# Prefetch hints on the closing branches, a shorter wait list on SyncE, and a row-sum check in two parts

## The chip, the cores and the metric

The kernel runs on one core of one Trainium2 chip. The metric is the device time of one execution in microseconds (us). Ratios below are the ratio of runs to the kernel before in the same comparison, with a 95% interval; they are not quite the ratio of the medians quoted beside them.

Terms: TensorE (PE, and PEld for its weight loads), VectorE (DVE), ScalarE (ACT), GpSimd (POOL) and SyncE (SP) are each given a program of their own. A "q" behind an engine's name in the profile means its sequencer: branches, waits, loads of registers. A P·V step multiplies the softmax weights by V (tile `ps_o`), a projection multiplies the result by `wo` (tile `ps_pj`), and a partial sum adds a projection to what was summed before; the last one of each half goes to the output buffer `ost`.

## The reference

Two attention layers side by side, their outputs concatenated:

```python
def _A_ref(x, k_cache, v_cache, wq, wo):        # 32 query heads share 4 key/value heads
    q = (x @ wq).reshape(B, Sq, Hq, Dh).transpose(0, 2, 1, 3)
    k, v = jnp.repeat(k_cache, rep, axis=1), jnp.repeat(v_cache, rep, axis=1)
    p = softmax(einsum("bhqd,bhkd->bhqk", q, k) * Dh ** -0.5)
    return einsum("bhqk,bhkd->bhqd", p, v).transpose(0, 2, 1, 3).reshape(B, Sq, Hq * Dh) @ wo
# _B_ref: the same with 32 key/value heads. B=16, Sq=32, D=1024, Sk=1024, Dh=128, bfloat16
return concatenate([a, b], axis=-1)
```

## The kernel before

The kernel holds two programs. The fast one computes softmax without subtracting the row maximum and records the reciprocal of every row sum in `rinv_all`. At its end a check asks whether all of these lie between 1e-10 and 1e10. If not, a general program computes everything again. With these inputs the check always passes, so every engine jumps over the general program, which lies between its fast program and the end.

The check, as it stands at the end of the fast program (cut):

```python
pr.add("dve", ... tensor_scalar(chk[:], rinv_all[:], RINV_LOW, None, ALU.is_ge, ALU.min, accum_out=good[:, 0:1]))
pr.add("dve", ... tensor_scalar(chk[:], rinv_all[:], RINV_HIGH, None, ALU.is_le, ALU.min, accum_out=good[:, 1:2]))
pr.add("pe",  ... matmul(ps_pj[0:1, 0:2], ones[:], good[:], start=True, stop=True))   # bank of the projections
pr.add("dve", ... tensor_tensor(good[0:1, 0:1], ps_pj[0:1, 0:1], good[0:1, 0:1], ALU.mult))
pr.add("dve", ... tensor_tensor(good[0:1, 1:2], ps_pj[0:1, 1:2], good[0:1, 0:1], ALU.mult))
pr.add("dve", ... tensor_copy(flag[:], good[0:1, 1:2]))
```

The closing of every engine's program:

```python
def whole(name, eng):
    fast.run_engine(name, eng, fast_sems)
    eng.wait_ge(fast_sems[flag_op.eng], flag_op.sig)
    reg = eng.alloc_register("flag_" + name)
    eng.reg_load(reg, flag[0:1, 0:1])
    if name == "sp":
        fast.await_dmas(eng, fast_sems)          # one wait for each of the DMA semaphores
    with eng.If_ne(reg, flag_good):
        ...                                      # meet the other engines, run the general program
```

The output goes out in eight stores of 128x1024 through one buffer `ost`, filled in two halves:

```python
pr.add("dve", ... tensor_tensor(o_ap, a_ap, ps_pj[:, 0:OUTW], ALU.add), writes=[BK_PJ, "ost"], name="accF")
...
pr.add("sp", ... dma_start(out_flat[...], ost[:, :]), reads=["ost"], dma_key=f"out{pi}")
```

The order on each engine is not the order of the source. A list scheduler reorders the whole fast program by the longest path to its end, so a changed check at the end can move instructions far ahead of it.

## Time and profile before

| | before |
|---|---|
| three runs | 858.39, 861.65, 861.66 us |
| span of the profiled run | 857.6 us |
| bytes moved, 0 to 820 us | 405 GB/s |
| bytes moved, 820 us to the end | 261 GB/s |
| last store issued | 851.72 us |
| last store issued to end of span | 5.88 us |

The body is bound by transfers (405 GB/s up to 820 us; the DMA engines stand at 9 tenths in 39 of the page's 40 slices); the change lies in the last six microseconds. The timeline there (start, duration, engine, line, operation, output from input, and in brackets the idle time before and what ended it):

```profile
851.00 0.69 DVE L725 TENSOR_TENSOR ost<-acc,ps_pj 128x512 bf16<-128x512 f32 x1 [1.70 <-PE ps_pj L709]
851.72 0.36 SPq L728 DMA_DIRECT2D out_dram<-ost  x1
...
851.75 0.19 PE L1108 MATMUL ps_pj<-good,ones 128*1 128x2 f32 x2 [0.78 <-DVE ost L725]
...
852.34 0.14 DVE L1114 CAST flag<-good 1x1 int32<-1x1 f32 x1
```

The check runs after the last store was issued, and the flag is there at 852.48. What follows is not engine work, so it is not in the timeline. It is in the view of single source lines (engine, operation, count, shortest/median/longest in ns, first and last start in us). The line of the branch:

```profile
L364 ACTq COMPARE_BRANCH  x1: 45/45/45, 853.3 to 853.3; - x1
L364 POOLq COMPARE_BRANCH  x1: 45/45/45, 853.3 to 853.3; - x1
L364 DVEq COMPARE_BRANCH  x1: 76/76/76, 853.3 to 853.3; - x1
L364 PEldq COMPARE_BRANCH  x1: 3648/3648/3648, 853.4 to 853.4; - x1
L364 SPq COMPARE_BRANCH  x1: 50/50/50, 854.5 to 854.5; - x1
```

SyncE's list of waits, the reason that its branch is 1.2 us later than the others:

```profile
L341 SPq EVENT_SEMAPHORE  x20: 28/28/28, 853.3 to 854.4; - x20
```

The first instruction behind the branch, a drain at the end of the block:

```profile
L355 POOLq DRAIN  x1: 41/41/41, 853.5 to 853.5; - x1
L355 ACTq DRAIN  x1: 80/80/80, 856.7 to 856.7; - x1
L355 DVEq DRAIN  x1: 57/57/57, 857.0 to 857.0; - x1
L355 PEldq DRAIN  x1: 73/73/73, 857.1 to 857.1; - x1
L355 SPq DRAIN  x1: 59/59/59, 857.3 to 857.3; - x1
```

The gap between branch and drain: 0.2 us on GpSimd, 2.8 to 3.7 us on the four others. On TensorE it is recorded as a long branch, on the others as nothing at all between two short instructions. I read the gap as a wait for the instructions of the branch target: packets of the instruction queues begin 0.9 to 1.1 us after these branches, 8 KB at 854.20, 854.40 and 855.45 us and 16 KB at 854.36. What the engines wait for in the rest of the gap the trace does not show.

The last store landed after 2.03 us. Its transfer, in the DMA view from issue to landing (40 slices of the stretch):

```profile
DMA  0000000000000000079799698996974200000000
GB/s 0 0 0 0 0 0 0 0 0 0 0 0 0 0 0 0 40 282 444 282 444 484 242 484 323 404 484 242 484 282 162 81 0 0 0 0 0 0 0 0
...
out_dram<-ost SPq DMA_DIRECT2D x1, 256.0 KB, 2.0
```

### The profile page before, as it was taken

Reading aid. Unit: us, or ns where it says so; the run is one execution under the profiler, and the core shown is the slowest. Engines: PE = TensorE matmul, PEld = TensorE weight load, DVE = VectorE, ACT = ScalarE, POOL = GpSimd, SP = SyncE. Lnnn points to the kernel's source line nnn. Section 1 sums busy time; section 2 is a strip of 40 time slices with the busy share of each in tenths; the row PEclk is TensorE's granted clock in tenths of the full one; section 3 lists DMA queues with packets and bytes.
Section 4 is the critical chain, followed back from the end, with each engine's and each line's share of the span. In section 5 each row is a group of like instructions: output and inputs, shape, how many; then the busy total and the mean of one; then the engine's idle time right before and its main releaser. Section 6 shows DMA issues by size and latency. Waiting matters only on the chain.

```text
span 857.6 us, 27298 instructions
## 1 busy us (share of the span) xinstructions
PE 717.3 (84%) x11970; PEld 436.2 (51%) x12098; DVE 541.5 (63%) x1115; ACT 447.1 (52%) x981; POOL 67.9 (8%) x76
## 2 busy tenths in 40 slices
PE   3999998898978789888897979988889778878885
PEld 2546655455545455555554545545455445545452
DVE  1655566666657477577674756757777656666674
ACT  1456766466544464546554545544565554555452
POOL 0001000100000000000000000000000000000000
PEclk9999999999999999999999989999999999999898
DMA  9999999999999999999999999999999999999994
GB/s 341 366 400 412 413 412 389 413 415 399 413 400 385 413 410 412 402 400 411 403 412 404 406 411 401 411 408 408 413 403 412 412 409 412 414 411 409 411 384 174
DMA packets 135547, 341.57 MB, mean 398 GB/s; under 512 B 10496, under 2 KB 26880, under 8 KB 119040
## 3 DMA queue, kind: packets, MB, share of 16 engines
q1 hardware_dynamic: 135424, 339.78, 101.1%
q8 instruction: 96, 1.57, 0.7%
q14 instruction: 27, 0.22, 0.1%
HBM read 337.64 MB, written 2.10 MB: 396 GB/s over the span
## 4 chain that ended last, share of the span: by engine, by line
DMA 53%; PE 19%; DVE 15%; SPq 6%; issue 4%; ACT 2%; POOL 1%; POOLq 0%; DVEq 0%
DMA KB_sb<-in_B_k_cache_dram 40%; DVE KBt_sb L820 12%; DMA VA_sb<-in_A_v_cache_dram 5%; PE ps_pj L709 4%; PE ps_s L855 3%; DMA woA_sb<-in_A_wo_dram 3%; PE ps_pj L651 3%; PE ps_pj L668 2%; SPq L800 2%; PE ps_o L947 2%; PE ps_kt L913 2%; SPq L682 1%; PE ps_s L838 1%; PE ps_pt L897 1%; DMA woB_sb<-in_B_wo_dram 1%
## 5 line engine op out<-in xcount | busy, mean ns | idle before, releaser
L820 DVE STREAM_TRANSPOSE KBt_sb<-KB_sb 128x1024 f32<-128x1024 f32 x256 | 306.1, 1226 | 97.7 <-DMA KB_sb<-in_B_k_cache_dram 93.9
L878 ACT ACTIVATE P_sb<-ps_s 128x512 bf16<-128x512 f32 x256 | 152.4, 600 | 84.1 <-PE ps_s L855 74.5
L870 ACT ACTIVATE PTA_sb<-ps_s 128x1024 bf16<-128x1024 f32 x128 | 131.3, 1026 | 104.2 <-PE ps_s L838 91.5
L855 PE MATMUL ps_s<-KBt_sb,QB_sb 32*32 32x512 bf16 x4096 | 146.9, 395 | 10.1 <-DVE KBt_sb L820 5.5
L582 ACT COPY PT_sb<-ps_pt 128x512 f32<-128x512 f32 x128 | 74.9, 585 | 105.7 <-PE ps_o L947 88.6
L794 POOL COPY VAp_sb<-VA_sb 128x1024 bf16<-128x1024 bf16 x64 | 66.6, 1041 | 761.9 <-DMA VA_sb<-in_A_v_cache_dram 729.4
L897 PE MATMUL ps_pt<-id,P_sb 128*128 128x128 f32 x512 | 105.5, 305 | 9.3 <-ACT P_sb L878 7.3
L947 PE MATMUL ps_o<-VB_sb,PT_sb 128*32 128x128 bf16 x4096 | 81.6, 221 | 23.7 <-DMA VB_sb<-in_B_v_cache_dram 16.6
L897 PEld LDWEIGHTS ps_pt<-id,P_sb 128*128 128x128 f32 x512 | 82.7, 206 | 35.2 <-ACT P_sb L878 17.7
L947 PEld LDWEIGHTS ps_o<-VB_sb,PT_sb 128*32 128x32 bf16 x4096 | 60.0, 97 | 60.2 <-issue 56.9
L913 PE MATMUL ps_kt<-VAp_sb,PTA_sb 128*128 128x129 bf16 x1024 | 80.8, 222 | 10.9 <-POOL VAp_sb L794 4.9
L913 PEld LDWEIGHTS ps_kt<-VAp_sb,PTA_sb 128*128 128x128 bf16 x1024 | 67.5, 99 | 36.5 <-POOL VAp_sb L794 14.9
L838 PE MATMUL ps_s<-QT_sb,KTA_sb 128*128 128x256 bf16 x512 | 82.2, 275 | 3.0 <-DVE KTA_sb L584 2.0
L855 PEld LDWEIGHTS ps_s<-KBt_sb,QB_sb 32*32 32x32 bf16 x4096 | 49.3, 90 | 60.9 <-DVE KBt_sb L820 10.6
L709 PE MATMUL ps_pj<-woA_sb,OTA_sb 128*128 128x512 bf16 x224 | 64.0, 394 | 17.4 <-DMA woA_sb<-in_A_wo_dram 10.0
L963 DVE TENSOR_SCALAR OB_sb<-ps_o,rinv_all 128x128 bf16<-128x128 f32 x128 | 43.7, 342 | 53.4 <-PE ps_o L947 52.6
L709 PE MATMUL ps_pj<-woB_sb,OTB_sb 128*128 128x512 bf16 x206 | 62.0, 394 | 16.6 <-ACT OTB_sb L582 4.5
L668 PE MATMUL ps_pj<-xT_sb,wq_sb 128*128 128x512 bf16 x234 | 64.2, 389 | 8.4 <-DMA wq_sb<-in_B_wq_dram 3.4
L651 PE MATMUL ps_pj<-xT_sb,wq_sb 128*128 128x512 bf16 x232 | 63.9, 380 | 8.3 <-DMA wq_sb<-in_A_wq_dram 4.1
L883 DVE TENSOR_TENSOR stat<-stat 64x1 f32<-64x1 f32 x256 | 41.9, 164 | 32.0 <-ACT P_sb L878 24.4
L838 PEld LDWEIGHTS ps_s<-QT_sb,KTA_sb 128*128 128x128 bf16 x512 | 45.0, 98 | 25.5 <-issue 4.4
L722 DVE TENSOR_TENSOR acc<-acc,ps_pj 128x512 f32<-128x512 f32 x64 | 43.0, 672 | 20.1 <-PE ps_pj L709 19.7
(49 smaller groups left out, 533.0 us busy)
## 6 DMA issues: line engine op xcount, KB each, us to landing
KB_sb<-in_B_k_cache_dram SPq DMA_DIRECT2D x128, 1024.0 KB, 9.1
VB_sb<-in_B_v_cache_dram SPq DMA_DIRECT2D x256, 512.0 KB, 9.8
KA_sb<-in_A_k_cache_dram SPq DMA_DIRECT2D x64, 256.0 KB, 10.3
VA_sb<-in_A_v_cache_dram SPq DMA_DIRECT2D x64, 256.0 KB, 9.6
wq_sb<-in_B_wq_dram SPq DMA_DIRECT2D x32, 256.0 KB, 8.6
wq_sb<-in_A_wq_dram SPq DMA_DIRECT2D x32, 256.0 KB, 8.5
woB_sb<-in_B_wo_dram SPq DMA_DIRECT2D x32, 256.0 KB, 10.8
woA_sb<-in_A_wo_dram SPq DMA_DIRECT2D x32, 256.0 KB, 10.1
```

Of the source, the lines that this page charges most:

```text
L582: pr.add("act", lambda e: e.copy(dst_ap, src_ap), reads=reads, writes=writes, name=name + "@act", wtag=wtag, rtag=rtag)
L651: last = e.matmul(ps_pj[:, 0:tn], wq_sb[:, 0, j, hc * Dh:(hc + 1) * Dh], xT_sb[:, 0, j, t0:t0 + tn], start=(j == 0), stop=(j == DJ - 1))
L668: last = e.matmul(ps_pj[:, 0:NTOK], w, xT_sb[:, 1, j, :], start=(j == 0), stop=(j == DJ - 1))
L709: last = e.matmul(ps_pj[:, 0:OUTW], OT[:, gp, hh, :], wo_[:, hh, oh * OUTW:(oh + 1) * OUTW], start=(hh == 0), stop=(hh == nh - 1))
L820: pr.add("dve", lambda e: e.transpose(KBt_sb[:, sl, t_, :].bitcast(F32).rearrange("p (s r i) -> p s r i", r=2, i=32), KB_sb[:, rs, t_, :]. ...
L838: last = e.matmul(ps_s[:, sbf, c2, i * 2 * P:(i + 1) * 2 * P], KTA_sb[:, sl, c * P:(c + 1) * P], qt, start=True, stop=True)
L855: last = e.matmul(ps_s[32 * cg:32 * cg + 32, sbf, g, :].rearrange("p (sh cl j) -> p sh cl j", sh=4, cl=4), lhsT, kt[32 * a:32 * a + 32, g, ...
L870: pr.add("act", lambda e: e.activation(dst, src, ACTF.Exp, scale=scale), writes=BK_S[sbf] + [("PTA", q.half)], name="expA", rtag={("Sv", s ...
L878: pr.add("act", lambda e, src=src, dst=dst, g=g: e.activation(dst, src, ACTF.Exp, scale=scale, accum_out=st[:, g:g + 1]), writes=[BK_S[sbf ...
L897: last = e.transpose(ps_pt32[:, m * P:(m + 1) * P], p32[:, m:Sk // 2:NPK], id32[:])
L913: last = e.matmul(ps_kt[:, qh * OA0:qh * OA0 + Dh + 1], PTA_sb[:, h, c, qh * P:(qh + 1) * P], VAp_sb[:, sl, 4 * h + c, 0:Dh + 1], start=(h ...
L947: last = e.matmul(ps_o[32 * a:32 * a + 32, 0:Dh], PT_pairs[:, c // 2, 32 * (a ^ (c // 4 * 2)):32 * (a ^ (c // 4 * 2)) + 32, c % 2], VB_sb[ ...
```

## The change

Its intent is to shorten the end: fetch the branch target ahead, let SyncE branch before it waits for the stores (and only for these), and have the flag ready before the last partial sums.

```diff
+NLATE = 8
-    def run_engine(self, eng_name, eng, sems):
+    def run_engine(self, eng_name, eng, sems, mark=None):
+        mine = [op for op in self.ops if op.eng == eng_name]
+        for k, op in enumerate(mine):
+            if mark is not None and k == max(0, len(mine) - mark[0]):
+                mark[1]()
...
+    stored = [k for k in sorted(fast.dma_count) if k.startswith("out")]
+    ahead = {"sp": 6, "pe": 60, "act": 12, "dve": 14, "pool": 3}
...
-            fast.run_engine(name, eng, fast_sems)
+            hints = []
+            fast.run_engine(name, eng, fast_sems, (ahead[name], lambda: hints.append(eng.mark_branch_hint_location())))
             eng.wait_ge(fast_sems[flag_op.eng], flag_op.sig)
             ...
-            if name == "sp":
-                fast.await_dmas(eng, fast_sems)
-            with eng.If_ne(reg, flag_good):
+            eng.br_ne(reg, flag_good, on_true=again, on_false=after).branch_hint(hints[0])
+            with nc.body(again, valid_engines=[eng.engine]):
+                if name == "sp":
+                    fast.await_dmas(eng, fast_sems, stored)
                 ...
+                eng.br(after)
+            nc.switch_bb(after)
+            if name == "sp":
+                fast.await_dmas(eng, fast_sems, stored)
...
+        # st_check_early, at step NIT - NLATE: the two comparisons over the columns of the first 120 steps
+        # st_check, at the end: the two comparisons over the last 8 steps, then
+                for k_ in range(4):
+                    last = e.matmul(ps_kt[0:1, 448:449], ones[:], good[:, k_:k_ + 1], start=(k_ == 0), stop=(k_ == 3))
+            pr.add("dve", lambda e: e.tensor_copy(flag[:], ps_kt[0:1, 448:449]), reads=[BK_KT], writes=["flag"], name="flag")
-            # one matmul into ps_pj, two products on VectorE, copy to the flag
-        emit_programs(nc, outer, pr, general, flag, P * P)
+        emit_programs(nc, outer, pr, general, flag, 4 * P)
```

`ahead` counts operations before the end of an engine's fast program.

More of the change, by code (lines that the diff above doesn't have):

```diff
@@ L325, in sem_names @@
         return ["pe", "act", "dve", "pool"] + sorted(self.dma_count.keys())
-    def run_engine(self, eng_name, eng, sems):
-        for op in self.ops:
-            if op.eng != eng_name:
-                continue
+    def run_engine(self, eng_name, eng, sems, mark=None):
[3 more added lines that the diff above has]
+                mark[1]()
             for key, val in op.waits:
@@ L337, in run_engine, with await_dmas @@
                 last.then_inc(sems[op.eng], 1)
-    def await_dmas(self, eng, sems):
-        for k, c in sorted(self.dma_count.items()):
-            eng.wait_ge(sems[k], 16 * c)
+    def await_dmas(self, eng, sems, keys):
+        for k in keys:
+            eng.wait_ge(sems[k], 16 * self.dma_count[k])
 def emit_programs(nc, stack, fast, general, flag, flag_good):
@@ L361, in whole @@
             eng.reg_load(reg, flag[0:1, 0:1])
-            if name == "sp":
-                fast.await_dmas(eng, fast_sems)
-            with eng.If_ne(reg, flag_good):
+            again, after = "again_" + name, "after_" + name
+            eng.br_ne(reg, flag_good, on_true=again, on_false=after).branch_hint(hints[0])
+            with nc.body(again, valid_engines=[eng.engine]):
+                if name == "sp":
+                    fast.await_dmas(eng, fast_sems, stored)
                 eng.drain().then_inc(meet, 1)
@@ L368, in whole @@
                 if name == "sp":
-                    general.await_dmas(eng, general_sems)
+                    general.await_dmas(eng, general_sems, sorted(general.dma_count))
+                eng.br(after)
+            nc.switch_bb(after)
+            if name == "sp":
+                fast.await_dmas(eng, fast_sems, stored)
         block.sync(lambda e: whole("sp", e))
@@ L531, in build @@
         chk = sb("chk", [P, 2 * NIT], BF)
-        good = sb("good", [P, 2], F32)
+        good = sb("good", [P, 4], F32)
         ones = sb("ones", [P, 1], F32)
@@ L973, in st_otr, with st_check, e_count, st_check_early @@
                  rtag={"OTps": q.qid}, wtag={("OTv", 1, gp): (q.m, q.G)} if q.last_of_group else None)
+        def st_check():
+            every = [("rinv_all", 0), ("rinv_all", 1)]
+            pr.add("pool", lambda g: g.memset(ones[:], 1.0), writes=["ones"], name="c0")
+            view = rinv_all[:, :].rearrange("p (i t) -> p i t", i=2)
+            outv = chk[:, :].rearrange("p (i t) -> p i t", i=2)
+            for k_, (bound, op) in enumerate(((RINV_LOW, ALU.is_ge), (RINV_HIGH, ALU.is_le))):
+                pr.add("dve", lambda e, k_=k_, bound=bound, op=op: e.tensor_scalar(outv[:, :, NIT - NLATE:], view[:, :, NIT - NLATE:], bound, None, op, ALU.min,
+                                                                               accum_out=good[:, 2 + k_:3 + k_]),
+                       reads=every, writes=["chk", ("good", 2 + k_)], name="check")
+            def e_count(e):
+                for k_ in range(4):
+                    last = e.matmul(ps_kt[0:1, 448:449], ones[:], good[:, k_:k_ + 1], start=(k_ == 0), stop=(k_ == 3))
+                return last
+            pr.add("pe", e_count, reads=["ones"] + [("good", k_) for k_ in range(4)], writes=[BK_KT], name="check")
+            pr.add("dve", lambda e: e.tensor_copy(flag[:], ps_kt[0:1, 448:449]), reads=[BK_KT], writes=["flag"], name="flag")
+            pr.add("pool", lambda g: g.memset(ones[:], 1.0), reads=["flag"], writes=["ones"], name="c0")
+        def st_check_early():
+            view = rinv_all[:, :].rearrange("p (i t) -> p i t", i=2)
+            outv = chk[:, :].rearrange("p (i t) -> p i t", i=2)
+            for k_, (bound, op) in enumerate(((RINV_LOW, ALU.is_ge), (RINV_HIGH, ALU.is_le))):
+                pr.add("dve", lambda e, k_=k_, bound=bound, op=op: e.tensor_scalar(outv[:, :, 0:NIT - NLATE], view[:, :, 0:NIT - NLATE], bound, None, op, ALU.min,
+                                                                               accum_out=good[:, k_:k_ + 1]),
+                       reads=[("rinv_all", 0), ("rinv_all", 1)], writes=["chk", ("good", k_)], name="check")
         quadsA = [mk_quadA(t) for t in range(NIT)]
@@ L1097, in build @@
             lazy_pop(LAZY_PER_STEP)
+            if t == NIT - NLATE:
+                st_check_early()
         cur_step[0] = 10 ** 9
         lazy_pop(1000)
-        def st_check():
-            every = [("rinv_all", 0), ("rinv_all", 1)]
-            pr.add("pool", lambda g: g.memset(ones[:], 1.0), writes=["ones"], name="c0")
-            pr.add("dve", lambda e: e.tensor_scalar(chk[:], rinv_all[:], RINV_LOW, None, ALU.is_ge, ALU.min, accum_out=good[:, 0:1]),
-                   reads=every, writes=["chk", ("good", 0)], name="check")
-            pr.add("dve", lambda e: e.tensor_scalar(chk[:], rinv_all[:], RINV_HIGH, None, ALU.is_le, ALU.min, accum_out=good[:, 1:2]),
-                   reads=every, writes=["chk", ("good", 1)], name="check")
-            pr.add("pe", lambda e: e.matmul(ps_pj[0:1, 0:2], ones[:], good[:], start=True, stop=True),
-                   reads=["ones", ("good", 0), ("good", 1)], writes=[BK_PJ], name="check")
-            pr.add("dve", lambda e: e.tensor_tensor(good[0:1, 0:1], ps_pj[0:1, 0:1], good[0:1, 0:1], ALU.mult),
-                   reads=[BK_PJ], writes=[("good", 0)], name="check")
-            pr.add("dve", lambda e: e.tensor_tensor(good[0:1, 1:2], ps_pj[0:1, 1:2], good[0:1, 0:1], ALU.mult),
-                   reads=[BK_PJ, ("good", 0)], writes=[("good", 1)], name="check")
-            pr.add("dve", lambda e: e.tensor_copy(flag[:], good[0:1, 1:2]), reads=[("good", 1)], writes=["flag"], name="flag")
-            pr.add("pool", lambda g: g.memset(ones[:], 1.0), reads=["flag"], writes=["ones"], name="c0")
         st_check()
```

## The prediction

What a hint does no trace had shown when this forecast was made: its 3.4 us per engine are the author's estimate from the gaps of 2.8 to 3.7 us above. The forecast's sum came to 3.5 us (857.6 less 854.1).

> **What bounds the kernel now.** Transfers. The page's slices show the DMA engines at 9 tenths nearly everywhere, 398 GB/s over the span; the chain that ended last is 53% DMA. From 0 to 820 us the windows show 405 GB/s. The change touches none of that. It touches the last 38 us (261 GB/s), really the last 6.
>
> **The end, from the timeline and the lines of the closing statements.** The last partial sum ends on VectorE at 851.69, the last store is issued at 851.72 and lands near 853.7 (stores of this window take 2.0 us). Then comes the check: matmul 851.75, three tiny VectorE operations, flag at 852.48. All five engines load the flag (0.72 to 0.80 us) and branch at about 853.3; SyncE first walks 20 more semaphore waits and branches at 854.50. From 853.4 to 857.6 no compute engine works. TensorE's branch lasts 3.65 us; the closing drains stand at 856.70 (ACT), 857.05 (DVE), 857.06 (PE), 857.34 (SP), but 853.50 for POOL, whose program is short. Packets of the instruction queues lie in that window. I read this as fetches of the branch target. [...] the trace agrees (2.8 to 3.7 us on four engines, none on POOL). The closing barrier takes 0.26 us.
>
> **What the change does.**
> - Hints, 3 to 60 operations ahead, should fetch the landing block during the tail: removes about 3.4 us per engine, in parallel.
> - SyncE waits for two stores instead of some 20 queues, after its branch: 1.2 us less before its branch.
> - The check splits: the first 120 steps' columns early (two VectorE operations of about 0.5 us, from 0.42+0.08 for 256 columns). Two products become four accumulating matmuls, in a bank that the output projection does not use; the flag is written before the last two partial sums: 0.8 us off the end.
>
> After this the last store should set the end: landing 853.7, drain and barrier 0.3, so about 854.1 against 857.6: **3.5 us saved, all on the critical path**.
>
> **Costs.** The four matmuls stand before the last P·V: perhaps 0.3 us (estimate from 0.19 us for two passes), mostly absorbed, since the next partial sum waits 1.9 us for the store that frees the output buffer. Hints: nothing visible. The list scheduler reorders the last third of the program, since the check's place in the graph changed; loads keep nearly the same order. I take this as neutral, plus or minus 2 us, as large as the effect.
>
> **Time.** Three runs gave 858.4, 861.65 and 861.66, so noise is as large as the gain. I predict 857.8 us, 853.5 to 861.5 holding it 8 times in 10. Chances: faster by over 2% 0.01, within 2% 0.98, slower 0.01.
>
> **What would show it.** TensorE's closing branch under 0.3 us; drains of ACT, DVE and PE well before SyncE's; SyncE's drain right after the last store lands; the end's instruction packets gone to 10 to 20 us earlier; last store issue to end of span 2.4 us, against 5.9. Last store issue at 851.7 plus or minus 2.
>
> **What would make it wrong.** A hint too early or too late is lost on one engine: its 3.4 us remain and only some 1 us is saved. SyncE's landing block ends in another branch, which may fetch again. The reordered schedule may cost or win more than the tail.

## The result, and the profile after

| | before | after |
|---|---|---|
| runs of the first comparison | 858.39 to 861.66, median 860.64 (4 runs) | 857.97 to 861.12, median 860.04 (4 runs) |
| ratio, 95% interval | 1 | 1.0002, 0.9978 to 1.0026 |
| second comparison (11 and 6 runs) | median 860.05 | median 859.14; ratio 0.9985, 0.9965 to 1.0005 |
| last store issued | 851.72 | 851.94 |
| last store issued to landed | 2.03 us | 3.11 us |
| last store issued to end of span | 5.88 us | 4.23 us |

The time is the same within the noise of the runs. The end became 1.65 us shorter, not 3.5. The branch and drain lines after:

```profile
L369 POOLq COMPARE_BRANCH  x1: 59/59/59, 847.9 to 847.9; - x1
L369 ACTq COMPARE_BRANCH  x1: 68/68/68, 848.8 to 848.8; - x1
L369 PEldq COMPARE_BRANCH  x1: 412/412/412, 850.7 to 850.7; - x1
L369 DVEq COMPARE_BRANCH  x1: 84/84/84, 851.8 to 851.8; - x1
L369 SPq COMPARE_BRANCH  x1: 75/75/75, 852.9 to 852.9; - x1
```

```profile
L360 PEldq DRAIN  x1: 62/62/62, 851.2 to 851.2; - x1
L360 ACTq DRAIN  x1: 81/81/81, 851.4 to 851.4; - x1
L360 DVEq DRAIN  x1: 58/58/58, 855.1 to 855.1; - x1
...
L360 SPq DRAIN  x1: 7/7/7, 855.9 to 855.9; - x1
```

TensorE's branch fell from 3.65 to 0.41 us. ScalarE still has 2.6 us between branch and drain, VectorE 3.3, SyncE 3.1. So one hint of the four that mattered worked.

SyncE ended last. The store had landed at 855.05, but the branch behind SyncE's waits for the stores is recorded at 855.76 only. From landing to end it took 1.12 us, against 0.50 us in e1 below, where SyncE's hint worked. So in this kernel the target that was missing on SyncE set the end.

The hints themselves (8 to 20 instructions ahead of the branch on all of these but TensorE):

```profile
L364 PEldq BRANCH_PREFETCH_HINT  x1: 45/45/45, 829.0 to 829.0; - x1
L364 ACTq BRANCH_PREFETCH_HINT  x1: 45/45/45, 830.3 to 830.3; - x1
L364 SPq BRANCH_PREFETCH_HINT  x1: 45/45/45, 830.9 to 830.9; - x1
L364 DVEq BRANCH_PREFETCH_HINT  x1: 51/51/51, 838.7 to 838.7; - x1
```

They were executed 18 to 22 us before the branches on the first three engines and 13 us on VectorE, which is more than the longest gap between branch and drain in any of these runs (4.1 us, TensorE in e9), and yet no packet of the small instruction queue follows until 849.70, after ScalarE's branch.

The second finding is in the last store's transfer, from issue to landing:

```profile
DMA  0300000000099898999520110500000000000000
GB/s 0 105 0 0 0 0 0 0 0 0 26 316 395 342 369 342 369 369 395 185 106 26 53 26 0 132 0 0 26 26 26 26 26 0 0 0 0 0 0 0
...
q14 instruction: 3, 0.02, 3.6%
...
out_dram<-ost SPq DMA_DIRECT2D x1, 256.0 KB, 3.1
```

Most of the store is through at the same pace as before, then a tail of single 2 KB packets follows (26 GB/s in a slice of 0.078 us is one such packet). Three instruction packets of 8 KB lie in the stretch, and one of 16 KB from TensorE's queue began just before it, at 851.82.

The single packets in the trace file tell which of them stands just before that tail. The 16 KB packet ended at 852.83, when the store's data had only just begun to move (852.80). One of the 8 KB packets ran from 852.85 to 853.66; it began 1.0 us after VectorE's branch. The tail is eight packets of the store's 128 of 2 KB. They follow each other from 853.66, the end of that packet, to 854.53, while all other data had moved by 853.76.

### The profile page after: what moved, and what is told of

Its sections match the earlier page's. It is cut to its first block, busy times and chain, and to the rows that moved or that the text cites. A ratio compares the mean times of both kernels' runs of the same rounds, so it can differ in the third digit from the quotient of the medians. Undisturbed runs are those within 1.5% of the kernel's fastest.

```text
span 856.2 us, 27420 instructions
## 1 busy us (share of the span) xinstructions
PE 730.4 (85%) x12104; PEld 433.8 (51%) x12104; DVE 541.8 (63%) x1117; ACT 447.6 (52%) x981; POOL 67.9 (8%) x76
## 4 chain that ended last, share of the span: by engine, by line
DMA 47%; PE 28%; DVE 17%; SPq 3%; issue 2%; ACT 2%; POOL 0%; DVEq 0%
DMA KB_sb<-in_B_k_cache_dram 29%; DVE KBt_sb L832 12%; DMA VB_sb<-in_B_v_cache_dram 7%; PE ps_pj L721 6%; PE ps_s L867 5%; DMA woA_sb<-in_A_wo_dram 4%; PE ps_o L959 3%; PE ps_pj L680 3%; PE ps_pj L663 3%; PE ps_kt L925 2%; DMA KA_sb<-in_A_k_cache_dram 2%; PE ps_pt L909 2%; PE ps_s L850 2%; DMA VA_sb<-in_A_v_cache_dram 1%; PE ps_kt L823 1%
## 5 line engine op out<-in xcount | busy, mean ns | idle before, releaser
L721 PE MATMUL ps_pj<-woB_sb,OTB_sb 128*128 128x512 bf16 x256 | 70.7, 385 | 12.4 <-DMA woB_sb<-in_B_wo_dram 4.7
L721 PE MATMUL ps_pj<-woA_sb,OTA_sb 128*128 128x512 bf16 x256 | 70.8, 391 | 11.6 <-DMA woA_sb<-in_A_wo_dram 9.8
L663 PE MATMUL ps_pj<-xT_sb,wq_sb 128*128 128x512 bf16 x256 | 70.3, 387 | 5.9 <-DMA wq_sb<-in_A_wq_dram 2.8
L680 PE MATMUL ps_pj<-xT_sb,wq_sb 128*128 128x512 bf16 x256 | 69.4, 393 | 5.3 <-DMA wq_sb<-in_B_wq_dram 3.5
```

The costliest lines, as they stand in the source:

```text
L663: last = e.matmul(ps_pj[:, 0:tn], wq_sb[:, 0, j, hc * Dh:(hc + 1) * Dh], xT_sb[:, 0, j, t0:t0 + tn], start=(j == 0), stop=(j == DJ - 1))
L680: last = e.matmul(ps_pj[:, 0:NTOK], w, xT_sb[:, 1, j, :], start=(j == 0), stop=(j == DJ - 1))
L721: last = e.matmul(ps_pj[:, 0:OUTW], OT[:, gp, hh, :], wo_[:, hh, oh * OUTW:(oh + 1) * OUTW], start=(hh == 0), stop=(hh == nh - 1))
```

## The experiments

All kernels gave the correct result. The first theory, formed from the two traces: a hint only tells the fetcher which block to load behind the block that holds the branch, and that load begins on entering the block. This is a guess, which the runs below test. It rests on a count of each engine's instructions at the moments of the packets. The queues do not name the engine, but the counts fit one 8 KB packet for each 128 instructions on ScalarE, VectorE and SyncE: in the changed kernel SyncE's go from its instruction 82 (81.4 us) to 593 in four steps, ScalarE's from 50 to 945 in seven, VectorE's from 49 to 1078 in eight. Their last regular fetches were at 808.2, 774.9 and 754.0 us, before their hints. TensorE's 95 packets of 16 KB up to 844.4 us go with 24,341 recorded instructions, 256 for each; the last of them, taken as its entry into the branch's block, came after its hint. "Block" below means such a stretch of 128 (TensorE: 256) instructions. The rival: only TensorE's fetcher obeys hints.

### e1: hints in the block before

```diff
-    ahead = {"sp": 6, "pe": 60, "act": 12, "dve": 14, "pool": 3}
+    ahead = {"sp": 100, "pe": 60, "act": 72, "dve": 150, "pool": 3}
```

> The changed kernel with the hints of SyncE, ScalarE and VectorE moved back by about 100 to 150 instructions, into the block of 128 instructions before the one that holds the branch; TensorE and GpSimd as they were. Theory 1 (a hint only changes which block is fetched next, and that fetch starts on entering the branch's block, so the hints of SyncE, ScalarE and VectorE came too late): their 2.6 to 3.2 us between branch and drain fall under 0.3 us, the instruction packets move from after the branch to 40 to 100 us before the end, SyncE's drain waits for the last store's landing only, last store issue to end falls from 4.23 to about 2.4 us; time about 2 us lower than the changed kernel, 0.4% under before. Rival (only TensorE's fetcher obeys a hint): nothing changes, 4.2 us.

Branch to drain fell to 0.48 us on ScalarE and 0.59 on VectorE (under 0.3 was expected). The rival is out.

```profile
L369 ACTq COMPARE_BRANCH  x1: 68/68/68, 849.6 to 849.6; - x1
L369 DVEq COMPARE_BRANCH  x1: 84/84/84, 852.6 to 852.6; - x1
...
L360 ACTq DRAIN  x1: 67/67/67, 850.1 to 850.1; - x1
...
L360 DVEq DRAIN  x1: 52/52/52, 853.2 to 853.2; - x1
```

The three fetches in the stretch from 740 to 812 us stayed three, at 754.4, 775.8 and 809.5: the hint adds no fetch there. That it changes what is fetched is my reading; the packets do not show their content. Behind 847 us the small instruction queue has 3 packets instead of 6. In the hint lines of e1, these now stand before the last regular fetches:

```profile
L364 SPq BRANCH_PREFETCH_HINT  x1: 45/45/45, 709.3 to 709.3; - x1
L364 DVEq BRANCH_PREFETCH_HINT  x1: 51/51/51, 748.8 to 748.8; - x1
L364 ACTq BRANCH_PREFETCH_HINT  x1: 45/45/45, 761.4 to 761.4; - x1
```

The expected 2.4 us from store to end was missed: it was 3.54. SyncE now waits for the store alone, but the store took 3.04 us to land. That was the second finding coming back, and it became a theory of its own (e7). Time: median 859.0 against 860.16, ratio 0.9986 (0.9958 to 1.0013).

### e2: TensorE's hint in the branch's own block

```diff
-    ahead = {"sp": 6, "pe": 60, "act": 12, "dve": 14, "pool": 3}
+    ahead = {"sp": 6, "pe": 8, "act": 12, "dve": 14, "pool": 3}
```

> The changed kernel with TensorE's hint moved from 577 to 68 instructions before the branch, into the branch's own block of 256. Theory 1: the hint is too late there as well, TensorE's branch takes 3 to 4 us again instead of 0.41. Rival (TensorE's fetcher obeys hints wherever they stand, the others never): still about 0.4 us. Last store issue to end stays at about 4.2 us by theory 1, since TensorE branches at about 850.7 and would drain at 854.3, before VectorE (855.1) and SyncE (855.9).

The first theory failed here. TensorE's branch took 0.49 us and its drain began 0.55 us after the branch. The late hint was not lost on TensorE (3.85 us without hints, e3). The hint stands at 847.15, and an extra packet of 16 KB follows 1.6 us later, at 848.75 (from 842 us on, TensorE's packets begin at 844.4 and 851.8 in the changed kernel, and at 845.6, 848.8 and 854.3 here). That packet fell into the store before the last, here from issue to landing:

```profile
GB/s 0 0 0 0 0 0 0 0 175 219 460 350 372 350 329 350 176 22 0 0 0 0 0 22 0 22 88 22 0 0 22 22 22 44 0 0 0 0 0 0
...
q8 instruction: 1, 0.02, 2.3%
```

The store's last eight packets start at 850.12, just as the 16 KB packet (848.75 to 850.13) ends; between 849.64 and 850.12 nothing of the store moves. The store was issued at 847.96 and landed after 3.73 us instead of 2.03, and the only output buffer was free that much later. In the waits of e2 from 847 to 856 us (who waited for whom, us in total, times, longest):

```profile
DVE ost L737 <- DMA out_dram<-ost: 3.4, 1, 3.4
```

From the third P·V step from the end to the last store it took 14.30 us, against 11.36 in the changed kernel. Of these 2.9 us, 1.7 are the slower store; another 0.8 are a last projection that took 1.89 us instead of 1.04, at a granted clock of 0.50 instead of 1.00 (why the clock fell is not tested). In this trace one 16 KB instruction fetch at the wrong moment went with 1.7 us more for a store.

### e3: the changed kernel without hints

```diff
-            eng.br_ne(reg, flag_good, on_true=again, on_false=after).branch_hint(hints[0])
+            eng.br_ne(reg, flag_good, on_true=again, on_false=after)
```

> The changed kernel without any hint. If the hints as placed gave nothing, last store issue to end stays at 4.2 us, TensorE's branch costs 3.6 us again but ends at about 854.3, off the path. If TensorE's hint was worth something, the end moves later by 0.5 us or more.

TensorE's branch took 3.85 us again, but its drain, at 852.80, came before SyncE's at 853.90. Last store to end was 3.99 us, not longer than the 4.23 of the changed kernel. The hints as placed gained nothing: the one that worked was on an engine that did not end last.

### e4: the split check alone, on the kernel before

```diff
-            eng.br_ne(reg, flag_good, on_true=again, on_false=after).branch_hint(hints[0])
...
+            if name == "sp":
+                fast.await_dmas(eng, fast_sems, sorted(fast.dma_count))
+            with eng.If_ne(reg, flag_good):
```

> The kernel before with the split check alone: SyncE waits for all queues before its branch, no hints. The flag is ready before the last partial sum, but SyncE issues the last store, loads the flag, walks 20 waits in about 1.2 us and branches at 2.2 us after the store's issue, then fetches for 2.8 us: last store issue to end about 5.2 us (before 5.88, changed kernel 4.23).

5.98 us, more than expected: SyncE's list of waits ended only with the store's landing, and the store took 2.80 us. SyncE branched 3.1 us after the issue, and its drain came 2.6 us behind the branch.

### e5: hints earlier, but inside the branch's block

```diff
-    ahead = {"sp": 6, "pe": 60, "act": 12, "dve": 14, "pool": 3}
+    ahead = {"sp": 55, "pe": 60, "act": 22, "dve": 86, "pool": 3}
```

> The changed kernel with the hints of SyncE, ScalarE and VectorE some 30 to 100 instructions ahead (about 30 to 100 us), but still behind the start of the 128-instruction block that holds the branch. If the block decides (the successor of the branch's block is already fetched by then), nothing is gained: branch to drain stays 2.5 to 3.3 us on ScalarE, VectorE and SyncE, and no instruction packet follows the hint. Rival (a hint needs lead, in time or instructions): the three gaps fall to about 0.5 us as with the far hints.

These hints came 30 us (ScalarE), 63 us (VectorE) and 89 us (SyncE) before their branches, and 10 to 15 us behind the last regular fetch of the engine:

```profile
L364 SPq BRANCH_PREFETCH_HINT  x1: 45/45/45, 764.3 to 764.3; - x1
L364 DVEq BRANCH_PREFETCH_HINT  x1: 56/56/56, 789.0 to 789.0; - x1
...
L364 ACTq BRANCH_PREFETCH_HINT  x1: 45/45/45, 818.1 to 818.1; - x1
```

The gaps stayed at 2.45, 3.16 and 3.09 us, and from 740 to 812 us the small instruction queue still has three packets. From 812 to 847 us it has none. So 30 to 89 us of lead did not help these hints. What sets them apart from those of e1 (0.48 and 0.59 us on ScalarE and VectorE) is that they came after the engine's last regular fetch, inside the branch's block.

### e6: hints two to three blocks ahead

```diff
-    ahead = {"sp": 6, "pe": 60, "act": 12, "dve": 14, "pool": 3}
+    ahead = {"sp": 240, "pe": 60, "act": 170, "dve": 330, "pool": 3}
```

> The changed kernel with those three hints two to three blocks ahead (240 to 370 instructions, 250 us and more). If the hint is kept until the fetcher comes to the branch's block, the gaps are about 0.5 us as with the far hints, and the last three fetches before the end stay where they were (about 753, 775 and 809 us). If it is carried out at once or forgotten, the gaps are 2.5 to 3.3 us again.

The gaps were 0.48 us (ScalarE) and 0.59 us (VectorE), with the hints at 644.2 and 612.7 us, over 200 us ahead; SyncE, hinted at 522.6, waited for the store only (landing to end 0.50 us, as in e1). I read this as a hint that is kept until its block comes; too early was no danger over this distance. The store again took 3.13 us to land, and store to end was 3.63.

### e7: far hints, and TensorE and VectorE branch later

Theory: a flag that is early lets engines branch early, and the instruction packets that begin about 1 us after a branch then fall into the last store. In the changed kernel VectorE branched at 851.82 us, an 8 KB packet ran from 852.85 to 853.66, and the store's last eight packets followed its end. By the theory an instruction packet holds back a part of the store for its own time (in the ends of the traces of before and after 0.3 to 0.8 us for 8 KB, 1.0 to 1.3 us for 16 KB). That it does so because both wait for the same DMA engine was the assumption; no trace here shows it.

```diff
+    last_dve = max(op.sig for op in fast.ops if op.eng == "dve" and op.sig is not None)
...
-            eng.wait_ge(fast_sems[flag_op.eng], flag_op.sig)
+            ready = last_dve if name in ("pe", "dve") else flag_op.sig
+            eng.wait_ge(fast_sems[flag_op.eng], ready)
```

> Far hints, and TensorE and VectorE load the flag only after the last partial sum is written, so that the block fetched behind their branch target is fetched about 0.8 us later. Theory (with the early flag, instruction packets fall into the last store and hold one of its packets back: the store took 3.11 us to land in the changed kernel and 3.04 with far hints, 2.03 before): the last store lands in 2.0 to 2.2 us again, and last store issue to end falls from 3.54 to about 2.55. Rival (the store is slow for another reason): it stays at 3.0 and 3.5.

The store landed in 2.03 us, and store to end was 2.53. The transfer from issue to landing in e7:

```profile
DMA  0000000000000000179899896998965109060000
GB/s 0 0 0 0 0 0 0 0 0 0 0 0 0 0 0 0 40 281 442 321 402 482 321 442 241 442 482 321 442 241 201 41 0 321 0 161 0 0 0 0
...
q8 instruction: 1, 0.02, 3.8%
...
out_dram<-ost SPq DMA_DIRECT2D x1, 256.0 KB, 2.0
```

The instruction packets are still there, but behind the store's data. That moving the fetches takes the extra microsecond away is shown (3.04 us to land in e1, 2.03 here); e7 moves those of TensorE and of VectorE together. Which of them mattered is read from the packets in the trace files. In every kernel whose last store landed late (after, e1 to e6, e11), a row of single store packets starts within 0.01 us of the end of an instruction packet, as if it had waited for that packet. In six of these eight (after, e1, e2, e5, e6, e11) the row that ends last follows an 8 KB packet that began 1.0 to 1.2 us after VectorE's branch. From this I take it that VectorE's small fetch, not TensorE's 16 KB, held these six stores back; no run moves one of the two alone. Time: median 857.59 against 859.42, ratio 0.9975 (0.9955 to 0.9996). It was run again below.

### e8: e7 with one output buffer for each half

```diff
-        ost = sb("ost", [P, D], BF)
+        ost = sb("ost", [P, 2, D], BF)
...                      # ost[:, pi, ...] in the partial sums and the store, key ("ost", pi) instead of "ost"
```

> The same with one output buffer for each half of the output, so that the partial sums of the last group no longer wait for the store before: the 2.0 us wait at about 844 us goes. Last P.V start of the pair before last to last store issue about 10.2 us instead of 11.2 to 11.4; last store issue to end 2.55 again. Time about 4 us below before, 0.995 of it.

Half a miss. The waits for the output buffer between 840 and 856 us went from 1.6 us in e7 (2.0 in the changed kernel) to none, and the landing stayed at 2.01. But from the start of the third P·V step from the end to the last store it took 11.87 us, not 10.2 (e7: 11.92). With the buffer free the scheduler put projections of the first half between the last P·V steps, and the chain of waits of e8 runs through TensorE there:

```profile
845.18 0.97 PE ps_pj L723 x4
...
847.53 0.56 PE ps_o L961 x32
848.10 0.97 PE ps_pj L723 x4
```

The wait became TensorE work on the chain. Ratio 0.9968 (0.9947 to 0.9988), not distinguishable from e7 on the same chip.

### e9: SyncE's new order alone, on the kernel before

```diff
-            if name == "sp":
-                fast.await_dmas(eng, fast_sems)
-            with eng.If_ne(reg, flag_good):
+            eng.br_ne(reg, flag_good, on_true=again, on_false=after)
...
+            nc.switch_bb(after)
+            if name == "sp":
+                fast.await_dmas(eng, fast_sems, stored)
```

> The kernel before with the order of SyncE alone changed: it branches first and then waits for the two store queues; no hints, check as before. SyncE branches at 1.6 us after the last store's issue instead of 2.8, but TensorE and VectorE branch at the same time (flag late) and need 3.7 us to their drains: last store issue to end about 5.6 us (before 5.88), so SyncE's waits were nearly off the path as long as the flag was late.

5.99 us, more than the 5.6 expected. All five engines branched at 853.6, and TensorE's branch took 4.00 us (3.65 in the kernel before, where SyncE branched 1.2 us later); its drain came last, at 857.72. SyncE's drain was earlier than before, 4.6 us after the store's issue instead of 5.6, and that was worth nothing.

### e10: e9 with far hints, the check left whole and late

```diff
+    ahead = {"sp": 100, "pe": 60, "act": 72, "dve": 150, "pool": 3}
...
-            eng.br_ne(reg, flag_good, on_true=again, on_false=after)
+            eng.br_ne(reg, flag_good, on_true=again, on_false=after).branch_hint(hints[0])
```

> The kernel before with SyncE's new order and working (far) hints, the check left whole, late and in the output projection's bank. Theory: with working hints the early flag is worth nothing, since all engines branch at about 1.6 us after the last store's issue, their next fetches begin behind the store's packets, and the store lands at 2.03: last store issue to end about 2.55 us, as with the split check and the later branch; ratio to before about 0.9965. Rival (the split check is needed for the gain): 3 us or more.

2.55 us, as expected. The flag comes 0.76 us after the last store's issue, all engines branch together, and the drains stand just around the landing at 854.64:

```profile
L358 ACTq DRAIN  x1: 67/67/67, 854.7 to 854.7; - x1
L358 PEldq DRAIN  x1: 62/62/62, 854.7 to 854.7; - x1
L358 DVEq DRAIN  x1: 52/52/52, 854.8 to 854.8; - x1
L358 SPq DRAIN  x1: 7/7/7, 854.9 to 854.9; - x1
```

Median 856.52 against 860.05 us, ratio 0.9962 (0.9934 to 0.9990). The gain over the kernel before is some 0.4%, with an interval clear of 1; beside the changed kernel on the same chip (e11, below, median 859.14) it is 2.6 us lower in the median.

### e11 and e12: the changed kernel and e7 again, beside e10

> The changed kernel as it is, timed again beside e10 and e12. From the traces it should be 1.65 us shorter than before at the end, ratio 0.998; last store issue to end 4.2 us, the store's landing 3.0 to 3.1 us.

> The kernel of e7 again, beside e10 and e11: last store issue to end 2.5 us, ratio to before about 0.996 and to the changed kernel about 0.998.

The changed kernel: median 859.14, ratio 0.9985 (0.9965 to 1.0005), store to end 4.17 us, landing 3.07. The kernel of e7: median 856.70, ratio 0.9969 (0.9944 to 0.9993), 2.52 us and 2.02. Both as expected.

The ladder of ends, last store issued to end of span, one trace each (e2, e5, e6 and e8 repeat a row of the table with 4.29, 4.25, 3.63 and 2.51 us):

| kernel | flag | SyncE branches first | hints that work | store landed | store to end |
|---|---|---|---|---|---|
| before | late | no | - | 2.03 | 5.88 |
| e4 | early | no | - | 2.80 | 5.98 |
| e9 | late | yes | - | 2.04 | 5.99 |
| e3 | early | yes | - | 2.85 | 3.99 |
| after (e11) | early | yes | TensorE | 3.11 (3.07) | 4.23 (4.17) |
| e1 | early | yes | all | 3.04 | 3.54 |
| e7 (e12) | early, TensorE and VectorE later | yes | all | 2.03 (2.02) | 2.53 (2.52) |
| e10 | late | yes | all | 2.02 | 2.55 |

## Why the prediction was right or wrong

- **The time** of 860.04 us lies in the predicted range of 853.5 to 861.5, and "within 2%" was right. The predicted 857.8 was 2.2 us too low. The range was wide because of the noise of the runs, and that judgement held: eleven runs of the kernel before in one comparison went from 857.9 to 864.3. A kernel without any gain would have met the range as well (860.64 us before), so the time being right says nothing for the mechanism.
- **"3.5 us saved, all on the critical path"** is the sum that failed: 1.65 us in the trace. From store issue to end 2.4 us were predicted and 4.23 measured. Of the difference, 0.7 us go with the hints (after to e1) and 1.0 us with the slow store (e1 to e7). Two of its terms were wrong.
- **"Hints, 3 to 60 operations ahead, should fetch the landing block during the tail: removes about 3.4 us per engine"** failed on ScalarE, VectorE and SyncE. Their hints stood in the branch's own block (2.6 to 3.3 us remained; e5: the same at 30 to 89 us of lead; e1 and e6: about 0.5 us with the hint in an earlier block). It was right on TensorE, where it was worth nothing (e3). The prediction had named this way of failing, "too early or too late is lost on one engine", but as a risk. It did not ask where the block boundaries lie, which the instruction packets of the trace of before already told (752.8, 771.9 and 808.9 us for the last 8 KB packets before the branches).
- **"Landing 853.7"**, that is 2.0 us after issue, was taken as fixed. The early flag moved instruction packets into the store, and it landed after 3.11 us. In the changed kernel SyncE's own gap of 3.1 us from branch to drain took still longer and hid this; once the hint worked, the store set the end (e1: 3.54 us, e7: 2.53).
- **"The flag is written before the last two partial sums: 0.8 us off the end"** was wrong as a gain. Alone it gives nothing (e4), and with working hints it is not needed (e10 against e7: 2.55 and 2.53 us). It counted where the hints are missing and SyncE branches first: e9 to e3, 5.99 to 3.99 us. TensorE's branch, 4.00 us long in e9 and 3.85 in e3, began 1.7 us behind the last store's issue in e9 and 1.2 us before it in e3.
- **"SyncE waits for two stores ... 1.2 us less before its branch"** was right: 2.8 us after the store's issue before, 0.9 us after, part of it from the early flag. With the late flag (e9) it is 1.6 us, so the shorter list is worth the predicted 1.2 there. Alone it is worth nothing (e9).
- **"Two products become four accumulating matmuls ... mostly absorbed"** was not separated by a run. In the changed kernel the next partial sum still came within 0.1 us of the landing of the store before. In the traces whose last projection took 1.04 us, the stretch from the third P·V step from the end to the last store was 11.18 to 11.71 us with the new check (after, e1, e3, e4, e6, e11, e12) and 11.32 and 11.76 us with the old one (e10, e9), so no cost shows.
- **The reordered schedule**, taken as "neutral, plus or minus 2 us", can be neither confirmed nor refuted to better than its own size. In ten traces of the changed kernel's order (after, e1 to e7, e11, e12) the third P·V step from the end began between 838.4 and 843.5 us, in three of the old order (before, e9, e10) between 839.9 and 841.3. The closest comparison is e10 (old order) with e12 (changed order), whose ends are alike: medians of 856.52 and 856.70 us, within the noise of each other.
- **SyncE's second branch**, feared to fetch again, took 0.05 us with the drain 0.2 us behind its start.

What stays open: why a late hint is followed by an extra 16 KB packet 1.6 us later on TensorE (e2) and by no packet on the others (e5). No run here tests that.

## What to carry to other kernels

Place a branch hint by fetch blocks, not by time: in this kernel, on ScalarE, VectorE and SyncE, it worked one to three blocks of 128 instructions before the one that holds the branch (e1, e6: 0.48 to 0.59 us from branch to drain on ScalarE and VectorE) and not inside that one (the changed kernel, e5: 2.45 to 3.3 us on the three). Parts that close a program in parallel were worth nothing one by one here (e4 and e9: 5.98 and 5.99 us against 5.88); ask for each engine when it branches, when its target is there, and which drain comes last. Instruction fetches are transfers like your data (1.79 of the 341.57 MB in the trace of before): a branch that is taken earlier than needed can send a fetch into the one store that everything waits for (here it landed after 3.11 instead of 2.03 us).
